# Cosine-weighted attention ahead of a routed expert layer: raw q transposed by plain products, k weighted on VectorE, and the K chunks spread evenly over the units

## The chip, the core and the metric

The kernel runs on one core of a Trainium2 chip. The metric is the device time of one execution in microseconds (us). The kernel before has a median of 337.25 us over three runs (336.64 to 337.82). The execution that was profiled took 336.46 us; its span from the first to the last instruction is 334.8 us.

Engines are named as in the profile: PE is TensorE (PEld its weight load), DVE is VectorE, ACT is ScalarE, POOL is GpSimd, SP is SyncE, which here only issues transfers.

## The reference

Eight batches of eight heads, 576 tokens of 64 values each, in float32. Attention without a softmax: q and k are rectified and weighted by a cosine and a sine of the token's place, k and v are contracted to a 128x64 matrix per head, and q is multiplied with it. Its output, 4608 rows of 512, goes through a layer in which each token uses the one of eight experts that its gate picks.

```python
def phi(x): r = np.maximum(x, 0.0); return np.concatenate([r * cos_w, r * sin_w], axis=-1)
kv  = np.einsum('bhsf,bhsd->bhfd', phi(k), v);  z = np.sum(phi(k), axis=2)
num = np.einsum('bhsf,bhfd->bhsd', phi(q), kv)
den = np.einsum('bhsf,bhf->bhs', phi(q), z)[..., None] + 1e-06
x   = num / den                                   # rows of 512: 8 heads x 64
e   = np.argmax(x @ w_gate, axis=1)               # one expert per token
out = softmax_e * sigmoid(x @ w_output_gate[:, e]) * (relu(x @ w1[e]) @ w2[e])
```

## The kernel before

Until about 158 us the kernel computes the attention, after that the expert layer. A batch of q, k or v lies in SBUF as 128 partitions x 4 head pairs x 9 chunks x 64 values: a partition holds nine neighbouring tokens of one head, and chunk c is the c-th of each nine.

**K side.** For each chunk, `kcs` holds the rectified k times the cosine (`k_cos`), and `tvs` holds v times the tangent with a column for the sum (`k_prep`). `k_piece` multiplies the two, and v itself, on PE, as 64x64 tiles; nine chunks add up in the PSUM tile `kvp`. In batches 2 to 7 both weightings are done by ACT, one chunk to an instruction (L342, L349). Then `g_cast` (DVE) and `g_keep` (ACT) copy `kvp` to SBUF, `g_tr` transposes it, and `g_mm` multiplies it with the gate weights, so that the query product yields the gate logits too.

**Q side.** A unit is a pair of chunks of one batch: four units for a batch, and a fifth after every odd batch for the ninth chunks of both. So a group, which is two batches, has nine units; there are four groups, 36 units. For a unit DVE rectifies q (`q_prep`, L492 and L496), PE transposes it as four 128x128 pieces against the identity (`q_tr`, L506), ACT copies the result out of PSUM (L509), PE multiplies with the matrix of the batch (`q_mm`, L530), ACT weights by the cosine (L535), and DVE adds the sine part (L537), which frees the PSUM tile `qo`; there are two of these. `q_out` makes the denominators on DVE and the rows of x on POOL (L556), and `route` picks experts. POOL writes the rows to their expert's place by indirect transfers (L658).

**What sets the order.** The program is written out by hand: each engine runs its instructions in the order in which the loop over the units emits them. In that loop (L975) unit i emits its own `q_mm`, the transposes of unit i + 2, the rectification of unit i + 3, the K products of the chunks that `after[i]` and `ahead[i]` list, and at its end the weightings (`preps`) for the next unit. The lists give three K chunks to a batch's first unit, two or three to the next ones, and the rest to the unit before its last. SP holds back each load of q, k or v until DVE has written the unit's `u` (L1066).

**Expert layer.** 39 slots of 128 tokens: `x_tr`, `layer1`, `h_tr`, `layer2`. The weights of the experts, 2 MB each, come through POOL's queue; the first transfer is issued behind unit 25 (L237), and DVE holds the first slots' copies back until the weights of the first two experts are there (L820).

Of the kernel before, what the change touches and what calls it, by code (L numbers as in the profile page):

```python
# [13 lines left out]
I32 = mybir.dt.int32  # L14
# [8 lines left out]
def kernel(  # L23
# [77 lines left out]
    kvcb, kvTb = own(512), own(512)  # L101
# [70 lines left out]
    def late_constants():  # L172
        DVE.tensor_copy(ident16[:], ident[:])
# [22 lines left out]

        prm_i = constp.tile([P, 6, E + 1], I32, name="prm_i")
# [9 lines left out]
        DVE.tensor_copy(prm[:], prm_i[:])  # L207
# [13 lines left out]


# [50 lines left out]
    if True:  # L273
# [59 lines left out]
        zm = wk.tile([P, 4, D], F32, name="zm", tag="zm", bufs=1)  # L333
        DVE.memset(zm[:], 0.0)
# [9 lines left out]
        def k_prep(b, cs):  # L344

            for c in cs:
                if b > 1:
                    k_cos(b, c, False)
                d = ACT.activation(tvs[:, c, :, 1:65], vbuf[b % 2][:, :, c, :], AF.Copy,  # L349
                                   scale=tanc[:, c:c + 1])  # L350
                tc.add_to_no_dep_group(f"tv{b}", d.ins)

# [27 lines left out]
        def k_piece(b, c, mh, outs, first):  # L380

            for mp in range(2):
                for i in range(2):
# [46 lines left out]
        def g_cast(b):  # L430
            for i in range(2):
                DVE.tensor_copy(kvcb[:, 256 * i:256 * i + 256].rearrange(
                    "p (m s w) -> p m s w", m=2, w=64), kv_of(b, i)[:, :, :, 0:64])

        def g_keep(b):
            new_kvm(b)
            for i in range(2):
                ACT.copy(ims(kvms[b][:])[:, i, :, :, 0:65], kv_of(b, i))

        def g0_evac(mh):  # L440
            if mh == 0:
                new_kvm(0)
            x = kvps[(0, mh)][:, :, 2:132].rearrange("p i (s w) -> p i s w", w=65)
            ACT.copy(ims(kvms[0][:])[:, :, mh, :, 0:65], x)
            DVE.tensor_copy(kvcb.rearrange("p (i m s w) -> p i m s w", i=2, m=2, w=64)[
                :, :, mh, :, :], x[:, :, :, 0:64])
# [4 lines left out]
        def g_tr(b, part=(0, 1)):  # L451
            tp = ptr.tile([P, 512], F32, name=f"kvtp{b}_{part[0]}", tag="tr")
            for qd in qds(part):
                PE.transpose(tp[:, 128 * qd:128 * qd + 128],
                             kvcb[:, 128 * qd:128 * qd + 128], ident[:])
# [29 lines left out]
        qrs = {}  # L485

        def q_prep(i):
            b, c = units[i]
            qb = qbuf[b % 2].rearrange("p m c d -> p c m d")
            if c < 4:  # L490
                qr = wk.tile([P, 2, 4, D], F32, name=f"qr{i}", tag="qr", bufs=2)
                DVE.tensor_scalar_max(qr[:], qb[:, 2 * c:2 * c + 2, :, :], 0.0)  # L492
                qrs[i] = qr
            if c == 4 or c == 3 and b % 2 == 0:
                qr = wk.tile([P, 4, D], F32, name=f"qrt{i}", tag="qrt", bufs=1)
                DVE.tensor_scalar_max(qr[:], qb[:, 8, :, :], 0.0)  # L496
                qrs[(i, 8)] = qr

        def q_tr(i):
            b, c = units[i]  # L500
            if c < 4:
                qr = qrs.pop(i)
                tp = ptr.tile([P, 512], F32, name=f"qtp{i}", tag="tr")
                for l in range(2):
                    for mh in range(2):
                        PE.transpose(toks(tp[:])[:, mh, :, l, :],  # L506
                                     qr[:, l, 2 * mh:2 * mh + 2, :].rearrange(
                                         "p m d -> p (m d)"), ident[:])
                ACT.copy(qT2[i % 2], tp[:])  # L509
            if c == 4 or c == 3 and b % 2 == 0:  # L510
                qr = qrs.pop((i, 8))
                tp = ptr.tile([P, 512], F32, name=f"qtt{i}", tag="tr")
                for mh in range(2):
                    PE.transpose(tp[:, 128 * mh:128 * mh + 128],
# [662 lines left out]
```

## Time and profile before

| | |
|---|---|
| median of three runs | 337.25 us (336.64 to 337.82) |
| profiled execution, and its span | 336.46 us, 334.8 us |
| busy over the span: PE, DVE, ACT, POOL | 286.1, 188.0, 156.4, 141.4 us |
| start, until the first unit's ACT work | 0 to 19.63 us |
| groups 0, 1, 2, 3 of the attention | 36.51, 34.30, 37.49, 30.22 us |
| from there to the end | 158.15 to 334.80 us |

A busy time is the time in which at least one instruction of the engine was under way. PE's matmuls overlap by their length in the pipeline, so a PE that reads as nine tenths busy can still have gaps; how long a row of matmuls takes is read from where it starts and where the next row starts. The stages above are cut where ACT begins with a group's first unit.

### The profile page before, as it was taken

The numbers are of one execution on the slowest core, as the hardware profiler recorded it, in microseconds if no ns is written. First come the engines' busy times: TensorE is split into PE (matmuls) and PEld (weight loads), VectorE is DVE, ScalarE is ACT, GpSimd is POOL, SyncE is SP. The second block draws the span as 40 slices with busy tenths as digits, with TensorE's granted clock in tenths as the row PEclk, the third lists the DMA queues.
The fourth block names the chain that finished last, engine by engine and source line by source line (L and its number), as shares of the span: only waits on it lengthen the run. The fifth ranks groups of instructions, "written<-read, shape, count | busy, mean of one in ns | idle before, by whom it ended". The sixth has DMA issues, their size and how long they took to land. (4 is left out here: it accounts for less than half of the span.)

```text
span 334.8 us, 10160 instructions
## 1 busy us (share of the span) xinstructions
PE 286.1 (85%) x3624; PEld 178.9 (53%) x3624; DVE 188.0 (56%) x548; ACT 156.4 (47%) x320; POOL 141.4 (42%) x184
## 2 busy tenths in 40 slices
PE   7859889888886878796958979988999999999980
PEld 3548777676665657663424545544554445444530
DVE  7484557567878989896668544434433323322330
ACT  3456889888979869752302212221232232223210
POOL 8003334328842776586677534242221322232231
PEclk9998999999999999998979999999999999999997
DMA  7997688678874877999998899999947777776811
GB/s 242 341 388 257 217 245 289 218 221 263 279 254 101 279 214 138 235 233 228 236 223 229 145 237 251 231 244 268 267 123 175 182 181 182 174 166 165 175 46 45
DMA packets 58208, 71.87 MB, mean 215 GB/s; under 512 B 23406, under 2 KB 38318, under 8 KB 58160
## 3 DMA queue, kind: packets, MB, share of 16 engines
q1 hardware_dynamic: 40608, 40.17, 42.6%
q0 software_dynamic: 17552, 31.05, 41.1%
q8 instruction: 32, 0.52, 0.7%
q14 instruction: 16, 0.13, 0.1%
HBM read 67.61 MB, written 16.17 MB: 250 GB/s over the span
## 5 line engine op out<-in xcount | busy, mean ns | idle before, releaser
L860 ACT ACTIVATE hs<-hp 128x1024 f16<-128x1024 f32 x39 | 39.9, 1023 | 118.3 <-PE hp L852 118.3
L852 PE MATMUL hp<-wt,xts 128*128 x312 | 75.3, 385 | 3.1 <-DVE xts L820 1.9
L870 PE MATMUL yps<-wt,hts 128*128 x312 | 74.9, 384 | 3.0 <-DVE ysb L877 1.5
L877 DVE TENSOR_SCALAR ysb<-yps,xg 128x512 f32<-128x512 f32 x39 | 29.3, 751 | 82.4 <-PE yps L870 82.4
L881 POOL DMA_INDIRECT out_dram<-ysb,sidx x31 | 30.2, 974 | 84.0 <-DVE ysb L877 81.9
L530 PE MATMUL qo<-kvm,wt 64*64 64x162 f32 x1024 | 43.4, 306 | 12.6 <-DVE wt L537 5.5
L870 PEld LDWEIGHTS <-hts 128*128 128x128 f16 x312 | 30.8, 99 | 40.9 <-issue 3.6
L537 DVE SCALAR_TENSOR_TENSOR wt<-qo,sinq,wt 128x324 f32<-128x324 f32 x72 | 36.8, 549 | 21.9 <-ACT wt L535 17.3
L852 PEld LDWEIGHTS <-xts 128*128 128x128 f16 x312 | 29.4, 99 | 32.2 <-issue 3.1
L535 ACT ACTIVATE wt<-qo,cosq 128x324 f32<-128x324 f32 x72 | 35.9, 536 | 17.6 <-PE qo L530 17.4
L530 PEld LDWEIGHTS qo<-kvm,wt 64*64 64x64 f32 x1024 | 34.9, 134 | 17.1 <-DVE wt L537 8.0
L392 PE MATMUL kvp<-wt 64*64 64x132 f32 x1080 | 38.3, 278 | 5.1 <-ACT wt L349 2.6
L556 POOL TENSOR_TENSOR xr<-wt,rc 128x512 f16<-128x512 f32 x36 | 38.0, 1062 | 6.4 <-DMA xs<-xr,di@1_0_1857 5.4
L392 PEld LDWEIGHTS kvp<-wt 64*64 64x64 f32 x1080 | 29.9, 132 | 12.4 <-ACT wt L349 7.1
L349 ACT ACTIVATE wt<-wt,tanc 128x256 f32<-128x256 f32 x63 | 31.6, 513 | 0.2 <-DMA wt<-in_v_dram 0.2
L573 POOL TENSOR_TENSOR gl<-wt,rc 128x256 f32<-128x256 f32 x12 | 7.6, 631 | 51.1 <-DVE rc L548 39.0
L342 ACT ACTIVATE wt<-wt,cosc 128x256 f32<-128x256 f32 x54 | 28.0, 518 | 0.0
L506 PE MATMUL qtp<-ident,qr 128*128 128x128 f32 x128 | 21.2, 288 | 3.7 <-DVE qr L492 2.0
L820 DVE COPY xts<-xtsp 128x512 f16<-128x512 f16 x39 | 16.3, 419 | 14.3 <-PE xtsp L804 4.8
L509 ACT COPY wt<-qtp 128x512 f32<-128x512 f32 x32 | 18.9, 589 | 5.9 <-PE qtp L506 5.7
L492 DVE TENSOR_SCALAR qr<-wt 128x512 f32<-128x512 f32 x32 | 19.6, 615 | 0.5 <-PE qtp L506 0.5
L506 PEld LDWEIGHTS qtp<-ident,qr 128*128 128x128 f32 x128 | 14.0, 143 | 8.9 <-DVE qr L492 3.4
(275 smaller groups left out, 303.3 us busy)
## 6 DMA issues: line engine op xcount, KB each, us to landing
wt<-in_moe_w_dram POOLq DMA_DIRECT2D x16, 1024.0 KB, 14.4
wt<-in_k_dram SPq DMA_DIRECT2D x16, 576.0 KB, 5.9
wt<-in_v_dram SPq DMA_DIRECT2D x16, 576.0 KB, 5.6
wt<-in_q_dram SPq DMA_DIRECT2D x16, 576.0 KB, 7.1
xg<-xs SPq DMA_DIRECT2D x43, 129.0 KB, 3.3
xs<-zt SPq DMA_DIRECT2D x9, 129.0 KB, 5.8
out_dram<-ysb,sidx POOLq DMA_INDIRECT x31, 2.9
hts<-hs SPq DMA_TRANSPOSE x19, 3.7
```

Source lines behind the costliest of these rows:

```text
L349: d = ACT.activation(tvs[:, c, :, 1:65], vbuf[b % 2][:, :, c, :], AF.Copy, scale=tanc[:, c:c + 1])
L392: mm = PE.matmul(outs(i, mp), kcs[rows, m, c, :], mov, start=first, stop=(c == NCH - 1), skip_group_check=True)
L506: PE.transpose(toks(tp[:])[:, mh, :, l, :], qr[:, l, 2 * mh:2 * mh + 2, :].rearrange("p m d -> p (m d)"), ident[:])
L530: PE.matmul(qo[64 * l:64 * l + 64, 2 * mp + ih, 0:162], qT[r, hf, ih, l, :], kvms[b if c < 4 else b - 1 + l][r, n0:n0 + 2, :], start=True, ...
L535: d0 = ACT.activation(t, qo[:, :, 0:81], AF.Copy, scale=cosq[:, c:c + 1])
L537: d1 = DVE.scalar_tensor_tensor(u[:, h0:h0 + 4, :], qo[:, :, 81:162], sinq[:, c:c + 1], t, ALU.mult, ALU.add)
L556: GP.tensor_tensor(xrows[:, slot + x, 0:DM].bitcast(F16).rearrange("p (h d) -> p h d", d=D), u[:, 8 * x:8 * x + 8, 0:64], rc[:, 8 * x:8 * ...
L852: mm = PE.matmul(hp[:, fh * 512:fh * 512 + 512], xts[:, kc, :], wt[:, bass.ds(ev, 1), kc * F + fh * 512:kc * F + fh * 512 + 512], start=(k ...
L860: ACT.activation(hs[:], hp, AF.Relu)
L870: mm = PE.matmul(yp, hts[:, fc, :], wt[:, bass.ds(ev, 1), 4 * F + fc * DM:4 * F + fc * DM + DM], start=(fc == 0), stop=(fc == 7))
L877: DVE.tensor_scalar(ysb[:], yp, xg[:, DM + 2:DM + 4].bitcast(F32), None, ALU.mult)
L881: d = GP.indirect_dma_start(out=out[:, :], out_offset=bass.IndirectOffsetOnAxis(ap=idx, axis=0), in_=ysb[:], in_offset=None, bounds_check= ...
```

## The change

- `q_prep` is gone. PE takes q as it was loaded: instead of four transposes of 128x128, `turn` makes eight plain products with the identity as the moving operand, each giving 64 of the 128 output partitions. ACT rectifies while it copies out of PSUM.
- `k_cos` runs on DVE for all batches from 1 on, once for all chunks of a unit: one instruction that takes the larger of k and zero and multiplies by a table `cosw` of 128x576, which POOL fills at the start. The weighting of v stays on ACT, but one chunk is given to DVE before the fourth and the ninth unit of a group.
- `g_cast` is gone. `g_keep` copies half of `kvp` on ACT and half on DVE, and `g_tr` transposes that copy, again by `turn`.
- The K chunks are spread over all units, mostly two to a unit, starting two units before the end of the group before for odd batches. The copy out of PSUM moves to the unit after the last chunk.
- Nine weightings of batch 1 and the constants that stood on DVE ahead of unit 0 are split: one weighting of two chunks stays there, the others go behind units 0 and 1, the constants into unit 4.
- Loads of q, k and v are issued up to two units earlier in a group; zeroed rows go out two to a unit; `q_sum` moves into `q_out`; the steps of the rank and table computation are dealt out differently.

```diff
-        def k_cos(b, c, dve):
-            kc = kbuf[b % 2][:, :, c, :]
-            if dve:
-                DVE.scalar_tensor_tensor(kcs[:, :, c, :], kc, cosc[:, c:c + 1], zm[:],
-                                         ALU.mult, ALU.max)
-            else:
-                ACT.activation(kcs[:, :, c, :], kc, AF.Relu, scale=cosc[:, c:c + 1])
+        def k_cos(b, cs):
+            c0, c1 = cs[0], cs[-1] + 1
...
+            DVE.scalar_tensor_tensor(
+                flat(kcs), flat(kbuf[b % 2]), 0.0,
+                cosw[:, c0 * D:c1 * D].unsqueeze(1).to_broadcast([P, 4, (c1 - c0) * D]),
+                ALU.max, ALU.mult)
...
+            for x, c in enumerate(cs):
+                v_, t_ = vbuf[b % 2][:, :, c, :], tvs[:, c, :, 1:65]
+                if x < on_dve:
+                    d = DVE.tensor_scalar(t_, v_, tanc[:, c:c + 1], None, ALU.mult)
+                else:
+                    d = ACT.activation(t_, v_, AF.Copy, scale=tanc[:, c:c + 1])
...
-            for i in range(2):
-                ACT.copy(ims(kvms[b][:])[:, i, :, :, 0:65], kv_of(b, i))
+            for i, copy in enumerate((ACT.copy, DVE.tensor_copy)):
+                copy(ims(kvms[b][:])[:, i, :, :, 0:65], kv_of(b, i))
...
+        def turn(out, in_):
+            PE.matmul(out, in_, ident[:], start=True, stop=True)
...
                 for l in range(2):
                     for mh in range(2):
-                        PE.transpose(toks(tp[:])[:, mh, :, l, :],
-                                     qr[:, l, 2 * mh:2 * mh + 2, :].rearrange(
-                                         "p m d -> p (m d)"), ident[:])
-                ACT.copy(qT2[i % 2], tp[:])
+                        for mp, to in enumerate(halves):
+                            turn(toks(tp[:])[to, mh, :, l, :],
+                                 qb[:, 2 * mh + mp, 2 * c + l, :])
+                ACT.activation(qT2[i % 2], tp[:], AF.Relu)
...
+            for b, plan in ((2 * g + 1, {-2: [0, 1], -1: [2, 3], 0: [4, 5], 1: [6, 7, 8]}),
+                            (2 * g + 2, {2: [0, 1], 3: [2, 3], 4: [4, 5], 5: [6, 7], 6: [8]})):
...
+                        after[9 * g + n] = (b, w)
...
-                step({20: 1, 21: 2, 22: 3, 23: 0, 24: 3, 25: 0, 26: 0}.get(i, 1))
+                step({20: 1, 21: 2, 22: 1, 23: 1, 24: 2, 25: 2}.get(i, 1))
```

DVE's order at the start, from the copy of the second half of batch 0 to the first unit's L537, in the kernel before:

```order
L477 COPY kvm_247<-kvgp_1_345 128x2x2x16
L339 SCALAR_TENSOR_TENSOR wt<-wt,cosc,zm 128x4x64 x9
L173 CAST ident_110<-ident 128x128
L186 CAST iota_114<-iota_i 128x8
L187 TENSOR_SCALAR iota8m<-iota_114 128x8
L188 TENSOR_SCALAR reg_116<-iota_114 128x8
L191 CAST iota_117<-iota_i 128x9
L194 CAST pv<-pv_i 128x1
L207 CAST prm<-prm_i 128x54
L209 TENSOR_TENSOR low<-iota_114 128x64
L213 TENSOR_TENSOR lt<-iota_114 128x64
L216 COPY base<-reg_116 128x8
```

And now, where `wt,cosw` marks the new weighting and L529 is the line that was L537:

```order
L480 COPY kvm_251<-kvgp_1_351 128x2x2x16
L339 SCALAR_TENSOR_TENSOR wt<-wt,cosw 128x4x128
L529 SCALAR_TENSOR_TENSOR wt<-qo_0_390,sinq,wt 128x324
L529 SCALAR_TENSOR_TENSOR wt<-qo_1_401,sinq,wt 128x324
L339 SCALAR_TENSOR_TENSOR wt<-wt,cosw 128x4x192
```

Nineteen instructions stood between that copy and the first unit's L537; one is left, and the other weightings follow behind.

ACT's order over one unit in the middle of a group, before, from one unit's two L535 to the next unit's (L342 and L349 weight k and v):

```order
L535 ACTIVATE wt<-qo_1_682,cosq 128x324
L509 COPY wt<-qtp_694 128x512
L342 ACTIVATE wt<-wt,cosc 128x4x64
L349 ACTIVATE wt<-wt,tanc 128x4x64
L342 ACTIVATE wt<-wt,cosc 128x4x64
L349 ACTIVATE wt<-wt,tanc 128x4x64
L535 ACTIVATE wt<-qo_0_735,cosq 128x324
```

The same place now (L527 is the former L535, L502 the former L509, L353 weights v):

```order
L527 ACTIVATE wt<-qo_0_1031,cosq 128x324
L527 ACTIVATE wt<-qo_1_1042,cosq 128x324
L502 ACTIVATE wt<-qtp_1053 128x512
L353 ACTIVATE wt<-wt,tanc 128x4x64 x3
L527 ACTIVATE wt<-qo_0_1093,cosq 128x324
```

The weightings of k have left ACT's queue.

PE's order over units 6 and 7, before (L530 is the query product, L514 and L506 the transposes of q, L454 that of the K matrix, L392 the K product):

```order
L530 MATMUL qo_1_807<-kvm_601,wt 64x162 x8
L514 MATMUL qtt_819<-ident,qrt_763 128x128 x2
L392 MATMUL kvp_702<-wt 64x132 x32
L530 MATMUL qo_0_867<-kvm_601,wt 64x162 x8
L530 MATMUL qo_1_878<-kvm_601,wt 64x162 x8
L454 MATMUL kvtp_0_889<-ident,wt 128x128 x4
L506 MATMUL qtp_895<-ident,qr_823 128x2x64 x4
```

The same two units now, and the K product behind unit 7 (L522 is the query product, L489 every `turn`, L399 the K product):

```order
L522 MATMUL qo_1_827<-kvm_595,wt 64x162 x8
L489 MATMUL qtt_838<-ident,wt 64x128 x4
L399 MATMUL kvp_648<-wt 64x132 x24
L522 MATMUL qo_0_880<-kvm_595,wt 64x162 x8
L522 MATMUL qo_1_891<-kvm_595,wt 64x162 x8
L489 MATMUL kvtp_0_902<-ident,kvm_877 64x128 x8
L489 MATMUL qtp_912<-ident,wt 64x2x64 x8
L399 MATMUL kvp_922<-wt 64x132 x16
```

Every piece to be transposed is now two products, and unit 7, which had no K product, has one of the next batch.

## Rows read from the trace of the kernel before

**Rows 1.** Busy time by stage: us, PE, PEld, DVE, ACT, POOL, PEclk, DMA share, GB/s.

```profile
19.63:56.14 36.51, 30.56 (x686) 25.39 (x682) 22.36 (x67) 28.41 (x67) 11.62 (x13) 0.95 0.82 262
56.14:90.44 34.30, 29.40 (x672) 23.43 (x668) 24.01 (x67) 29.69 (x73) 18.82 (x23) 1.00 0.79 250
90.44:127.93 37.49, 28.97 (x656) 22.97 (x649) 31.96 (x96) 30.28 (x73) 22.51 (x25) 1.00 0.68 214
127.93:158.15 30.22, 24.81 (x486) 18.62 (x485) 25.60 (x76) 19.00 (x46) 19.91 (x22) 0.98 1.11 215
...
175.00:334.80 159.80, 143.74 (x866) 73.08 (x863) 61.34 (x154) 36.83 (x36) 49.68 (x53) 0.99 0.81 184
```

**Rows 2.** ACT in order of time, group 1: start, us, line, tile.

```profile
70.75 0.51 ACT L342 ACTIVATE wt<-wt,cosc 128x256 f32<-128x256 f32 x1
...
73.17 0.93 ACT L535 ACTIVATE wt<-qo,cosq 128x324 f32<-128x324 f32 x2
```

**Rows 3.** Waits of groups 1 and 2: engine, line, waited for; us, times, longest.

```profile
PEld kvp L392 <- ACT wt L349: 4.0, 10, 0.8
...
PE qo L530 <- DVE kvm L475: 2.5, 1, 2.5
```

**Rows 4.** PE in order of time, group 1: start, us until the last result.

```profile
77.22 1.13 PE L392 MATMUL kvp<-wt 64*64 64x132 f32 x32
78.17 1.28 PE L530 MATMUL qo<-kvm,wt 64*64 64x162 f32 x32
79.39 0.44 PE L514 MATMUL qtt<-ident,qrt 128*128 128x128 f32 x2
...
84.48 0.60 PE L506 MATMUL qtp<-ident,qr 128*128 128x128 f32 x4
85.01 1.33 PE L530 MATMUL qo<-kvm,qTt 64*64 64x162 f32 x32
86.27 0.66 PE L469 MATMUL kvgp<-wpr,wt 128*64 128x32 f32 x16
```

**Rows 5.** PE's L469 under way or done by 86.34 us, by 86.37 us.

```profile
86.27 0.25 PE L469 MATMUL kvgp<-wpr,wt 128*64 128x32 f32 x2
86.27 0.31 PE L469 MATMUL kvgp<-wpr,wt 128*64 128x32 f32 x4
```

**Rows 6.** DVE's groups in group 1: count, busy us, mean ns, idle before.

```profile
L492 DVE TENSOR_SCALAR qr<-wt 128x512 f32<-128x512 f32 x8 | 4.3, 543 | 0.0
...
L432 DVE COPY wt<-kvp 128x256 f32<-128x256 f32 x4 | 1.5, 418 | 1.2 <-PE kvp L392 1.1
...
L496 DVE TENSOR_SCALAR qrt<-wt 128x256 f32<-128x256 f32 x2 | 1.5, 736 | 0.0
```

**Rows 7.** The same line L492 in group 2.

```profile
L492 DVE TENSOR_SCALAR qr<-wt 128x512 f32<-128x512 f32 x8 | 6.1, 760 | 0.0
```

**Rows 8.** L573 on DVE over the span: ns min/median/max.

```profile
L573 DVE TENSOR_TENSOR gl<-wt,rc x8: 291/425/1771, 55.1 to 166.2; 128x128 f32<-128x128 f32 x4, 128x256 f32<-128x256 f32 x4
```

**Rows 9.** DVE in order of time, ahead of unit 0 and in it.

```profile
18.56 3.65 DVE L339 SCALAR_TENSOR_TENSOR wt<-wt,cosc,zm 128x256 f32<-128x256 f32 x9 [0.41 <-DMA wt<-in_k_dram]
...
23.19 1.01 DVE L537 SCALAR_TENSOR_TENSOR wt<-qo,sinq,wt 128x324 f32<-128x324 f32 x2
24.12 0.41 DVE L492 TENSOR_SCALAR qr<-wt 128x512 f32<-128x512 f32 x1
```

**Rows 10.** PE in order of time, units 1 and 3.

```profile
23.79 2.29 PE L530 MATMUL qo<-kvm,wt 64*64 64x162 f32 x32 [3.09 <-DVE wt L537]
...
33.43 1.28 PE L530 MATMUL qo<-kvm,wt 64*64 64x162 f32 x32
```

**Rows 11.** ACT's first weighting of v of batch 1.

```profile
21.61 1.30 ACT L349 ACTIVATE wt<-wt,tanc 128x256 f32<-128x256 f32 x3 [0.24 <-DMA wt<-in_v_dram]
```

**Rows 12.** POOL: the first transfer of expert weights.

```profile
127.23 0.83 POOL L237 DMA_DIRECT2D wt<-in_moe_w_dram  x1
```

**Rows 13.** DVE: the first slots' copies, held back for the weights.

```profile
156.48 0.75 DVE L820 COPY xts<-xtsp 128x512 f16<-128x512 f16 x2 [2.23 <-DMA wt<-in_moe_w_dram]
```

More of the change, by code (lines that the diff above doesn't have):

```diff
@@ L100 @@
     kbuf[1] = mcd(own(HW))
-    kvcb, kvTb = own(512), own(512)
+    kvTb = own(512)
     qbuf[0] = mcd(own(HW))
@@ L206, in late_constants @@
         GP.memset(prm_i[:, 5, E:E + 1], E - 1)
+        for m, i in ((GC, 0), (GC, 1), (4, 1), (5, 1)):
+            t = constp.tile([P, m + 1, E], F16, name=f"oh16_{m}_{i}")
+            GP.memset(t[:, m, :], 0.0)
+            oh16s[(m, i)] = t
+    def late_constants():
+        DVE.tensor_copy(ident16[:], ident[:])
+        DVE.tensor_copy(iota8[:], iota8_i[:])
+        DVE.tensor_scalar_add(iota8m[:], iota8[:], -8.0)
+        DVE.tensor_scalar_mul(reg0[:], iota8[:], float(REG))
+        DVE.tensor_copy(iota9[:], iota9_i[:])
+        DVE.tensor_copy(pv[:], pv_i[:])
         DVE.tensor_copy(prm[:], prm_i[:])
@@ L331, in place_gates, with flat, k_prep @@
                             :, :, 2 * ab:2 * ab + 2, :])
-        zm = wk.tile([P, 4, D], F32, name="zm", tag="zm", bufs=1)
-        DVE.memset(zm[:], 0.0)
-        def k_cos(b, c, dve):
-            kc = kbuf[b % 2][:, :, c, :]
-            if dve:
-                DVE.scalar_tensor_tensor(kcs[:, :, c, :], kc, cosc[:, c:c + 1], zm[:],
-                                         ALU.mult, ALU.max)
-            else:
-                ACT.activation(kcs[:, :, c, :], kc, AF.Relu, scale=cosc[:, c:c + 1])
[L344 to L350, printed above, removed]
+        cosw = wk.tile([P, NCH * D], F32, name="cosw", tag="cosw", bufs=1)
+        def k_cos(b, cs):
+            c0, c1 = cs[0], cs[-1] + 1
+            def flat(x):
+                return x[:, :, c0:c1, :].rearrange("p m c d -> p m (c d)")
+            DVE.scalar_tensor_tensor(
+                flat(kcs), flat(kbuf[b % 2]), 0.0,
+                cosw[:, c0 * D:c1 * D].unsqueeze(1).to_broadcast([P, 4, (c1 - c0) * D]),
+                ALU.max, ALU.mult)
+        def k_prep(b, cs, on_dve):
+            if b > 1:
+                k_cos(b, cs)
+            for x, c in enumerate(cs):
[4 more added lines that the diff above has]
+                    d = ACT.activation(t_, v_, AF.Copy, scale=tanc[:, c:c + 1])
                 tc.add_to_no_dep_group(f"tv{b}", d.ins)
+                for x_ in range(NCH):
+                    if x_ != c:
+                        tc.declare_no_dep(d.ins, group=f"mm{b - 1}_{x_}",
+                                          reason="of another chunk")
         def k0_prep(hf):
@@ L443, in g0_evac @@
             x = kvps[(0, mh)][:, :, 2:132].rearrange("p i (s w) -> p i s w", w=65)
-            ACT.copy(ims(kvms[0][:])[:, :, mh, :, 0:65], x)
-            DVE.tensor_copy(kvcb.rearrange("p (i m s w) -> p i m s w", i=2, m=2, w=64)[
-                :, :, mh, :, :], x[:, :, :, 0:64])
+            for i, copy in enumerate((ACT.copy, DVE.tensor_copy)):
+                copy(ims(kvms[0][:])[:, i, mh, :, 0:65], x[:, i])
         def qds(part):
@@ L453, in g_tr @@
             for qd in qds(part):
-                PE.transpose(tp[:, 128 * qd:128 * qd + 128],
-                             kvcb[:, 128 * qd:128 * qd + 128], ident[:])
+                for s in range(2):
+                    turn(tp[64 * s:64 * s + 64, 128 * qd:128 * qd + 128],
+                         kvms[b][:, 2 * qd + s, 0:64])
             def pick(x):
@@ L483, in toks @@
             return x.rearrange("p (m i l t) -> p m i l t", m=2, i=2, l=2)
[L485 to L497, printed above, removed]
+        def turn(out, in_):
+            PE.matmul(out, in_, ident[:], start=True, stop=True)
         def q_tr(i):
             b, c = units[i]
+            qb = qbuf[b % 2]
+            halves = (slice(0, 64), slice(64, 128))
             if c < 4:
-                qr = qrs.pop(i)
                 tp = ptr.tile([P, 512], F32, name=f"qtp{i}", tag="tr")
@@ L949 @@
         g_tr(0, (1,))
-        q_prep(0)
-        q_prep(1)
         q_tr(0)
-        q_prep(2)
         g_mm(0, (1,))
-        q_tr(1)
-        for c in range(NCH):
-            k_cos(1, c, True)
-        late_constants()
+        k_cos(1, [0, 1])
+        pool_constants()
         pending = []
@@ L1068 @@
                 f(*x)
-            if 3 <= i <= 3 + E:
-                zero_rows(i - 3)
+            if 3 <= i <= 7:
+                for e in range(2 * i - 6, min(2 * i - 4, E + 1)):
+                    zero_rows(e)
             if i == 19:
```

100 lines of the change are left out of this document (42 added, 58 removed).

## The prediction

> **What bounds it now.** I read the busy times by stage first [rows 1]. From 175 us on PE is busy 143.7 of 159.8 us; the change touches nothing there, so any gain has to come from the attention, 19.63 to 158.15 us. In groups 0 and 1 the fullest engine beside PE is ACT (28.4 of 36.5 us, 29.7 of 34.3), in group 2 DVE (32.0 of 37.5) with ACT close behind (30.3). In group 3 the DMA share is 1.11.
>
> PE's 29 us per group are not a measure, since its records overlap. The order of time shows what PE needs when nothing holds it [rows 4]: 32 K products (two chunks) 0.95 us from their start to the next start (77.22 to 78.17), a unit's 32 query products 1.22 with the changeover behind them (78.17 to 79.39), four transposes 0.53 with the changeover back (84.48 to 85.01), which I split into 0.44 and 0.09; 16 gate products 0.59 (the busy 0.66 less the end of the last one). A group has nine units, 18 K chunks, eight sets of four and two of two for q, two of four for kv, two gate products: 9 x 1.22 + 9 x 0.95 + 8 x 0.44 + 2 x 0.22 + 2 x 0.44 + 2 x 0.59 + 9 x 0.09 for the changeover back + about 0.3 for the ranks = 26.6 us. Group 1 took 34.3, so PE waits nearly 8 us in it. The waits say for whom [rows 3]: K products for ACT's v, the query product for the gate columns. ACT is the common cause: in units with three chunks it runs six weightings in a row, 0.40 us from start to start (70.75 to 73.17) [rows 2], with the next unit's L535 behind them.
>
> **ACT.** 18 L342 a group at 0.40 us, 7.2 us [rows 2], leave its queue; two weightings of v and half of the copies out of `kvp` go too. ACT falls to about 21 of 34 us and bounds nothing. Relu in place of a plain copy out of PSUM I take as free: L342, a Relu, has the same spacing as the weighting of v beside it [rows 2].
>
> **PE.** A set of four transposes becomes eight products of 64 columns. Each is two records, as every plain float32 product here (the order lists 16 L392 for two chunks, the trace 32), and streams 128 columns. Per set of four tiles 132 columns take 0.95/8 = 0.119 us with the end of the row, so 128 take about 0.11. Whether the two 64-column halves run beside each other decides: beside, 8 pairs x 0.11 = 0.89 us; in a row, 16 x 0.11 = 1.78. The one row of that shape is the gate product: by 86.34 us two have started, by 86.37 four [rows 5], so they start in pairs. I take 0.89, 0.45 more than now, and keep 0.44 and 1.78 as ends. A group then needs 26.6 + 8 x 0.45 + 2 x 0.22 + 2 x 0.45 - 0.2 (gate products and transposes no longer change over) = 31.3 us. That is the new floor, below each of the three groups' times.
>
> **DVE.** Removed in group 1: L492, L496 and L432, 4.3 + 1.5 + 1.5 = 7.3 us [rows 6]. Added: nine weightings for 18 chunks. One chunk now takes 0.40 (3.65 us for nine, the last result included) [rows 9]; DVE's tensor products grow by about 1.05 ns per element (128 to 256 elements, 291 to 425 ns) [rows 8], so two chunks take 0.67, three 0.93. One triple, seven pairs and a single are 6.0 us; two copies at 0.36 and two weightings of v, for which I take 0.3 each, make 7.3. DVE stays at 24 us in group 1 and 31 in group 2 (where 6.1 of L492 go [rows 7]). The bounds for one pair: 0.41, what DVE's fastest form needs for 512 elements, and 0.75 plus a wait for POOL (rival 1).
>
> That wait is real today. L492 takes 0.41 us alone [rows 9], 0.54 on average in group 1 and 0.76 in group 2 [rows 6, 7], where POOL is busy 22.5 us; L573 takes 1.77 us at worst instead of 0.29 [rows 8]. I let the nine weightings inherit what L492 pays now, so it cancels.
>
> The Trainium skill, "SBUF — State Buffer", section "Who interferes with whom", says that a VectorE instruction with two SBUF inputs is blocked for the whole of a GpSimd instruction that reads SBUF; the new weighting has two, k and `cosw`. L573, also with two, agrees; by this rule alone each weighting could pay a full wait, which is rival 1.
>
> **The start.** PE waits 3.09 us in unit 1 for L537 [rows 10], which stands behind the nine weightings and the constants until 23.19 [rows 9]. With one pair ahead of it (0.75 us from 18.56) it follows L535 at about 20.2. What is late next is v of batch 1: its first weighting waits for the transfer until 21.61 [rows 11], the first K product comes at 22.4, unit 1's query product at 23.4 instead of 23.79. From there to unit 3 PE needs 2 x 1.22 + 2 x 0.98 + 0.44 + 7 x 0.475 = 8.2 us against 9.64 now (23.79 to 33.43; the query product there took 2.29 us instead of 1.28) [rows 10]. So unit 3 starts 1.9 us earlier. Units 3 to 8 have little to gain: PE's sum for them comes to about 22 us, as long as they take now. Start and group 0: -2.0 us.
>
> **Groups 1 and 2.** With even K chunks ACT and DVE have their work for a unit done before PE wants it, and the gate columns get a K product's time to arrive; PE's waits go, its own sum stays. Group 1: 31.3 plus 0.7 of remaining waits, 32.0, -2.3 us. In group 2 the rank and table steps sit on DVE in lumps, and DVE has 31 us of work beside PE's 31.3; I take the middle between 31.3 and 37.5, 34.4. Eight ninths of that gain fall ahead of the first weight transfer: -2.7.
>
> **Group 3 and the end.** The first transfer of weights starts at 127.23 [rows 12], and the first slots wait for weights until 156.48 [rows 13], with the DMA engines full [rows 1]. These 29.3 us are bytes, not engine time; I carry them over unchanged, and all that follows. The gain is what unit 25 gains. PE and DVE will be done earlier in group 3 and wait longer.
>
> **At nothing.** `cosw` is made on POOL while the first loads run and is first wanted at 18.6 [rows 9]; I put its worst at 1 us. Zeroed rows two to a unit and loads one or two units earlier go past SP's hold on `u`; groups 0 and 1 have a DMA share of about 0.8. Worst 1 us in group 0. The reduction of the gate sums moves behind a POOL result that is then two units old.
>
> **Sum.** -2.0 - 2.3 - 2.7 = -7.0 against the profiled 336.46: 329.5 us. The median shown is 0.8 above that execution, so 330.3 in its terms.
>
> **Rivals.** 1. Slower: the weightings collide with POOL. If each of nine waits out a POOL instruction, 1.77 - 0.29 = 1.48 us, DVE has 24.0 + 13.3 = 37.3 us in group 1 and 44.4 in group 2: +3.0, +6.9 x 8/9, less 2.0 at the start (POOL is idle there) = +7.1, 344. It decides from a wait of (34.3 - 24.0)/9 = 1.1 us each in group 1. For it speaks the 1.77, against it the means of L492, 0.13 and 0.35 above its undisturbed time. Chance 0.11.
> 2. Slower: the halves don't overlap. PE then has 31.3 + 12 x 0.89 - 0.9 = 41 us a group: +6.7, +3.2, and some 7 in group 0: 353. Against it the pairs in [rows 5]. Chance 0.04.
> 3. It trades one wait for another: PE's longer turns and DVE's weightings fill what ACT sets free, groups 1 and 2 stay near their times, the start remains: 335.3, spread 333 to 338. Speaks for it: DVE at 32 of 37.5 keeps all its work. Chance 0.17.
> 4. More: the weights land earlier too, because fewer other bytes are under way when they start, and group 3 (PE's own sum there, by the same prices, is about 26 of 30.2 us) gives back 4 us: 326. Against it the DMA share of 1.11. Chance 0.15.
> The forecast itself has 0.53, with 327 to 334.
>
> **Numbers.** Under 0.3% (1 us) a measurement of this kernel can't tell a difference from none. Faster: 0.53 + 0.15 + 0.10 of rival 3 = 0.78; same 0.07; slower 0.11 + 0.04 = 0.15. The range 324 to 337.5 leaves out rivals 1 and 2 and the edges of 3 and 4, under 0.2.
>
> **What would show it.** Turns of eight products that last 0.9 us (1.8 would be rival 2); pair weightings of 0.75 us, under 1.1 on average (2.2: rival 1); group 1 in 32 us with ACT busy about 21; no wait of 3 us in unit 1; the first slots' wait for weights longer than 2.2 us and still 29 us behind the first transfer. Wrong it is if group 1 takes 34 us or more, or if the attention's gain is lost in the wait for weights.

## The result and the profile after

The kernel after takes 340.48 us (median of 20 runs, 335.64 to 342.75), the kernel before 336.53 us beside it (20 runs, 333.59 to 339.34): 1.0103 of its time, 95% interval 1.0069 to 1.0137. It is slower by 1.0%. (The ratio leaves out executions that took over 1.5% more than their kernel's fastest; the medians of all 20 stand at 1.0117.) I had forecast 330.3 us and 324 to 337.5. The profiled execution of after has a span of 339.0 us, 4.2 more than that of before.

The windows of after by stage, cut where the first ScalarE weighting of units 0, 9, 18 and 27 starts and the last unit's result ends, as in [rows 1] (width, then busy us and count of PE, weight loads, DVE, ACT, POOL, clock, DMA share, GB/s):

```profile
18.95:57.02 38.07, 35.55 (x872) 31.03 (x868) 24.18 (x59) 25.69 (x55) 14.12 (x14) 1.00 0.84 291
57.02:91.90 34.88, 32.65 (x802) 28.25 (x798) 26.12 (x67) 22.99 (x51) 20.52 (x21) 1.00 0.66 229
91.90:129.80 37.90, 33.01 (x802) 28.15 (x798) 34.63 (x96) 23.37 (x50) 23.54 (x25) 1.00 0.58 198
129.80:161.68 31.88, 27.31 (x537) 20.81 (x530) 24.80 (x70) 16.39 (x35) 20.15 (x21) 1.00 1.10 209
175.00:338.00 163.00, 148.99 (x877) 75.55 (x875) 61.38 (x154) 36.91 (x37) 52.21 (x55) 0.97 0.83 184
```

Every group is longer than in [rows 1]: +1.56, +0.58, +0.41 and +1.66, together +4.21 us. That is one execution of each. The same program, run again as experiment 9, took 37.6, 34.8 and 39.2 us in groups 0 to 2, and experiment 8, whose group 1 is that of after, took 37.2 us in it. So no single group's difference is shown by these rows; their sum fits the medians. Unit 0 starts 0.68 earlier (19.63 to 18.95), and from the last unit's end to the end of the span it is 177.3 us instead of 176.7. The same rows say how the four groups grew. PE is busy 128.5 us in them instead of 113.7, 14.8 more. The time in which it is not busy falls from 24.8 to 14.2 us, 10.6 less. So waits did go, but fewer than half of them where I had forecast nearly all, and more PE work came in than waits went out. ACT fell from 29.7 to 23.0 us in group 1, much as forecast, and the group got no shorter.

PE of after in order of time, two units of group 1 (start, us, what):

```profile
70.17 1.28 PE L522 MATMUL qo<-kvm,wt 64*64 64x162 f32 x32
71.38 0.66 PE L472 MATMUL kvgp<-wpr,wt 128*64 128x32 f32 x16
71.87 1.07 PE L489 MATMUL qtp<-ident,wt 128*64 128x128 f32 x16
72.87 1.13 PE L399 MATMUL kvp<-wt 64*64 64x132 f32 x32
```

A turn takes 1.00 us from its start to the next start (71.87 to 72.87); four transposes took 0.53 (84.48 to 85.01 in [rows 4]). That is 0.47 more a unit, where I had 0.45. The Trainium skill, "Perfetto Trace Analysis", section "Transposes", says that a logical transpose should use the transpose operation rather than a plain matrix product; the trace agrees, by these 0.47 us. It speaks against this change, and I had not weighed it.

The waits of after, of group 1 first (us in total, times, longest) and then of group 2:

```profile
ACT wt L527 <- PE qo L522: 4.5, 9, 0.9
DVE wt L529 <- ACT wt L527: 2.9, 3, 1.1
...
PE kvtp L489 <- DVE kvm L441: 0.7, 1, 0.7
```

```profile
ACT wt L527 <- PE qo L522: 4.9, 8, 1.1
...
PE kvtp L489 <- DVE kvm L441: 2.7, 2, 2.0
PE kvp L399 <- DVE wt L339: 2.1, 3, 1.2
```

No product of PE waits for ACT any more in these two groups; ACT now waits for PE's query product in most units. In group 2 PE is idle for 4.89 us, and 4.8 of them are waits for DVE, for its half of the kv copy and for the new weighting of k. In group 1 PE is idle for 2.23 us, in three places ("issue" is a pause for which the profile names nothing that was waited for):

```profile
58.61 1.09 PE L489 MATMUL qtp<-ident,wt 128*64 128x128 f32 x16 [1.11 <-issue]
67.76 0.66 PE L489 MATMUL kvtp<-ident,kvm 128*64 128x128 f32 x8 [0.71 <-DVE kvm L441]
75.50 0.49 PE L522 MATMUL qo<-kvm,wt 64*64 64x162 f32 x5 [0.42 <-issue]
```

So two thirds of what was left are pauses of the first kind. Group 1 of the kernel before had them too:

```profile
PE kvp L392 <- issue: 1.0, 1, 1.0
PE qtp L506 <- issue: 0.7, 1, 0.7
```

That weighting over the whole kernel (min, median, max ns), and then DVE and POOL around the longest unit, 25:

```profile
L339 DVE SCALAR_TENSOR_TENSOR wt<-wt,cosw x29: 410/682/2303, 18.5 to 135.3; 128x512 f32<-128x512 f32 x21, 128x768 f32<-128x768 f32 x5, 128x256 f32<-128x256 f32 x2, 128x1024 f32<-128x1024 f32 x1
```

```profile
121.86 0.68 DVE L339 SCALAR_TENSOR_TENSOR wt<-wt,cosw 128x512 f32<-128x512 f32 x1
122.47 0.42 DVE L441 COPY kvm<-kvp 128x260 f32<-128x260 f32 x1
...
125.44 1.55 DVE L339 SCALAR_TENSOR_TENSOR wt<-wt,cosw 128x512 f32<-128x512 f32 x1
```

```profile
124.80 0.63 POOL L566 TENSOR_TENSOR gl<-wt,rc 128x256 f32<-128x256 f32 x1 [2.02 <-DVE glog L573]
125.39 1.06 POOL L549 TENSOR_TENSOR xr<-wt,rc 128x512 f16<-128x512 f32 x1
...
128.89 0.83 POOL L235 DMA_DIRECT2D wt<-in_moe_w_dram  x1
```

Two chunks take 0.68 us in the first row and 1.55 where POOL's L549 began 0.05 us earlier. Of the 21 weightings of two chunks five took over 1 us (1.05 to 2.30), each with an L549 under way in it. The last line is the first transfer of weights, 1.66 later than in [rows 12]. The copies that wait for it start at

```profile
160.00 0.75 DVE L813 COPY xts<-xtsp 128x512 f16<-128x512 f16 x2 [2.35 <-DMA wt<-in_moe_w_dram]
```

31.1 us behind it, against 29.3 from [rows 12] to [rows 13]. They wait for the weights of two experts, and POOL issues the second expert's first transfer 12.6 us behind the first expert's (11.6 before, 127.23 to 138.82), after a wait for DVE's denominators:

```profile
139.30 2.29 POOL L549 TENSOR_TENSOR xr<-wt,rc 128x512 f16<-128x512 f32 x2 [6.29 <-DVE rc L540]
141.53 0.82 POOL L235 DMA_DIRECT2D wt<-in_moe_w_dram  x1
```

So about 1 of these 1.8 us comes from the order of the engines and not from the transfers.

### The profile page after: what moved, and what is told of

Same layout as the page of the kernel before. It is cut to its first block, busy times and chain, and to the rows that moved or that the text cites. A ratio compares the mean times of both kernels' runs of the same rounds, so it can differ in the third digit from the quotient of the medians.

```text
span 339.0 us, 11125 instructions
## 1 busy us (share of the span) xinstructions
PE 300.8 (89%) x4152; PEld 197.6 (58%) x4152; DVE 193.2 (57%) x526; ACT 136.7 (40%) x253; POOL 147.7 (44%) x185
## 3 DMA queue, kind: packets, MB, share of 16 engines
q1 hardware_dynamic: 40608, 40.17, 41.1%
## 5 line engine op out<-in xcount | busy, mean ns | idle before, releaser
L853 ACT ACTIVATE hs<-hp 128x1024 f16<-128x1024 f32 x39 | 39.9, 1023 | 118.3 <-PE hp L845 118.3
L863 PE MATMUL yps<-wt,hts 128*128 x312 | 76.1, 388 | 1.7 <-DVE ysb L870 1.5
L870 DVE TENSOR_SCALAR ysb<-yps,xg 128x512 f32<-128x512 f32 x39 | 29.3, 750 | 83.9 <-PE yps L863 83.9
L527 ACT ACTIVATE wt<-qo,cosq 128x324 f32<-128x324 f32 x72 | 37.4, 530 | 20.8 <-PE qo L522 20.2
L529 DVE SCALAR_TENSOR_TENSOR wt<-qo,sinq,wt 128x324 f32<-128x324 f32 x72 | 36.9, 548 | 14.2 <-ACT wt L527 10.2
L522 PE MATMUL qo<-kvm,wt 64*64 64x162 f32 x1024 | 43.1, 299 | 2.0 <-issue 1.0
L399 PE MATMUL kvp<-wt 64*64 64x132 f32 x1080 | 38.0, 277 | 6.9 <-ACT wt L353 2.2
L549 POOL TENSOR_TENSOR xr<-wt,rc 128x512 f16<-128x512 f32 x36 | 39.6, 1106 | 6.6 <-DVE rc L540 6.3
L399 PEld LDWEIGHTS kvp<-wt 64*64 64x64 f32 x1080 | 30.4, 132 | 12.8 <-issue 7.2
L522 PEld LDWEIGHTS qo<-kvm,wt 64*64 64x64 f32 x1024 | 35.2, 132 | 4.5 <-issue 2.4
L489 PE MATMUL qtp<-ident,wt 128*64 128x128 f32 x512 | 34.5, 277 | 1.1 <-issue 1.1
L566 POOL TENSOR_TENSOR gl<-wt,rc 128x256 f32<-128x256 f32 x12 | 9.4, 786 | 55.2 <-DVE glog L573 20.3
L489 PEld LDWEIGHTS qtp<-ident,wt 128*64 128x64 f32 x512 | 27.8, 137 | 5.1 <-issue 5.1
L502 ACT ACTIVATE wt<-qtp 128x512 f32<-128x512 f32 x32 | 19.1, 596 | 17.7 <-PE qtp L489 16.8
L353 ACT ACTIVATE wt<-wt,tanc 128x256 f32<-128x256 f32 x57 | 25.7, 501 | 0.4 <-DVE wt L339 0.4
L339 DVE SCALAR_TENSOR_TENSOR wt<-wt,cosw 128x512 f32<-128x512 f32 (+3 forms) x29 | 25.1, 866 | 0.6 <-DMA wt<-in_k_dram 0.6
L797 PE MATMUL xtsp<-ident,xg 128*128 128x128 f16 x156 | 15.2, 222 | 3.6 <-DMA xg<-xs 3.6
```

The lines of the kernel that those rows point to most:

```text
L353: d = ACT.activation(t_, v_, AF.Copy, scale=tanc[:, c:c + 1])
L399: mm = PE.matmul(outs(i, mp), kcs[rows, m, c, :], mov, start=first, stop=(c == NCH - 1), skip_group_check=True)
L489: PE.matmul(out, in_, ident[:], start=True, stop=True)
L522: PE.matmul(qo[64 * l:64 * l + 64, 2 * mp + ih, 0:162], qT[r, hf, ih, l, :], kvms[b if c < 4 else b - 1 + l][r, n0:n0 + 2, :], start=True, ...
L527: d0 = ACT.activation(t, qo[:, :, 0:81], AF.Copy, scale=cosq[:, c:c + 1])
L529: d1 = DVE.scalar_tensor_tensor(u[:, h0:h0 + 4, :], qo[:, :, 81:162], sinq[:, c:c + 1], t, ALU.mult, ALU.add)
```

## The experiments

The kernel before was run in every job, and its median went from 336.5 to 343.4 us between jobs. So I compare ratios, and kernels of one job with each other where I can. But the other kernels moved less: experiments 12 and 13 are the same kernel in two jobs, 334.14 and 334.54 us, and experiment 6, which lacks two small edits of theirs, took 334.62 where before took 343.18. A ratio to a before of 343 us is therefore too favourable, and after itself was never run beside one. Theory A: PE's own added work bounds groups 0 and 1, DVE's weighting groups 2 and 3. Theory B: DVE's weighting alone is the cause.

**1. The price of the turn.**

```diff
-  for mp, to in enumerate(halves):
-      turn(toks(tp[:])[to, mh, :, l, :], qb[:, 2 * mh + mp, 2 * c + l, :])
+  PE.transpose(toks(tp[:])[:, mh, :, l, :],
+               qb[:, 2 * mh + l, 2 * c:2 * c + 2, :].rearrange("p c d -> p (c d)"), ident[:])
```

> The kernel after, but each 128x128 block of q is turned by one whole-width transpose of 128 contiguous columns (two chunks of one head) in place of two 64-wide products; the data land in the wrong arrangement, so the output is not the reference's, while every other instruction and every transfer is as in the kernel after. Theory A (TensorE's own work sets the pace: the turn of 16 records takes 0.82 us a unit where four transposes took 0.38 to 0.44): 32 units x 0.43 plus 8 tail blocks x 0.17 = 15 us come off TensorE, part of it returns as waits; 326 to 333 us, group 1 at 30 to 33 us. Theory B (VectorE's wide k weighting beside GpSimd sets the pace, 25 us of it at a mean of 866 ns): not more than 2 us gained, 337 us or more.

Measured 357.06 us, 1.0565 (1.0505 to 1.0626). The total can't be read here: the wrong rows are routed unevenly, and from the start of unit 35 to the end it takes 203 us instead of 181. The attention can: units 0 to 35 take 133.6 us instead of 139.2. Its windows:

```profile
18.68:54.68 36.00, 32.12 (x752) 27.62 (x748) 24.59 (x58) 25.85 (x55) 13.88 (x14) 0.95 0.91 295
54.68:86.40 31.72, 29.03 (x694) 24.33 (x690) 25.55 (x68) 22.99 (x50) 19.69 (x21) 1.00 0.74 253
86.40:125.53 39.13, 31.12 (x694) 25.64 (x690) 35.81 (x98) 23.26 (x51) 25.29 (x27) 0.96 0.63 203
```

Groups 0 and 1 get 2.1 and 3.2 us shorter, group 2 gets 1.2 longer: theory A in the first two, and something else, with DVE busy 35.8 us, in the third.

**2. The turn alone, in the kernel before.** The same eight products and Relu in the copy; VectorE's `q_prep` taken out.

> The kernel before with one part of the change: raw q turned by products of 64 columns and rectified in ScalarE's copy, VectorE's rectifying copy gone; k weighting, kv copies, K stream, loads and start as before. Theory A: TensorE gains 15 us of work over 32 units, its waits of 32 us in the four groups hide part of it; 340 to 346 us against 336.5, TensorE's floor in group 1 from 26.7 to 30.6 us. Theory B: the turn is hidden and VectorE is relieved of 8 copies of about 0.54 us a group: 332 to 336.5 us.

Four runs, 339.48 to 345.55 us, median 343.14 against 336.91, without an interval: within theory A's forecast. The profiled one has 36.0 us in group 1 (34.3 before) and 37.4 in group 2 (37.5). The turn is not hidden, and DVE's relief returns nothing in groups 0 and 1.

**3. k weighted on ScalarE again, in the kernel after.**

```diff
-  DVE.scalar_tensor_tensor(flat(kcs), flat(kbuf[b % 2]), 0.0, ..., ALU.max, ALU.mult)
+  for c in cs:
+      ACT.activation(kcs[:, :, c, :], kbuf[b % 2][:, :, c, :], AF.Relu, scale=cosc[:, c:c + 1])
```

> The kernel after, but k is weighted chunk by chunk on ScalarE again (one activation of 128x256 a chunk), so that VectorE sheds 25 us of weighting and ScalarE takes up some 28 us. Theory A: TensorE's floor of 31.7 us in group 1 stays, and so do 337 to 345 us. Theory B: the pace was VectorE's: 328 to 335 us.

336.89 us beside 336.91, 0.9971 (0.9921 to 1.0021): between the two forecasts. Group 1 is not shorter than in after (35.7 us), groups 2 and 3 are (36.7 and 30.0). Each theory holds for half the program, as far as one execution tells.

**4. The pairs made by the load.** q written as `p (c m d)`, in runs of 64 floats, and four whole transposes of raw q.

> The kernel after with q laid out by its load so that the two heads of a pair stand side by side (written in runs of 64 floats), and raw q turned by four whole transposes a unit; still rectified in ScalarE's copy. The output is the reference's. Theory A: as the whole-width turn, 326 to 333 us, if the transfers of 256-byte runs stay hidden; if they do not, waits for q appear in the first units of a batch and the time is 340 us or more. Theory B: 337 us or more without any wait for q.

344.67 us, 1.0212 (1.0157 to 1.0267). The loads don't stay hidden. The queue of the loads (packets, MB, share of the engines' time), and the longest wait for one, in units 10 and 11:

```profile
q1 hardware_dynamic: 73632, 40.17, 46.1%
```

```profile
ACT wt L358 <- DMA wt<-in_v_dram: 6.1, 1, 6.1
```

The bytes are those of after, in 73,632 packets instead of 40,608, and 46.1% of the engines' time instead of 41.1%. It is v, behind q in the same queue, that comes 6.1 us late. SP shows part of the way: it takes 6.47 us over issuing the four transfers of q ahead of it, where after takes 0.90 over its two, and this v goes out at 60.28 us instead of 54.72 (unit 8 starts at 54.9 instead of 53.4).

```profile
48.78 6.47 SPq L296 DMA_DIRECT2D wt<-in_q_dram  x4
60.28 0.43 SPq L299 DMA_DIRECT2D wt<-in_v_dram  x1
```

```profile
47.51 0.90 SPq L292 DMA_DIRECT2D wt<-in_q_dram  x2
54.72 0.37 SPq L292 DMA_DIRECT2D wt<-in_v_dram  x1
```

**5. The turn undone, the weighting kept.** `q_prep` and the transposes of before put into the kernel after.

> The kernel after with the turn of q undone: VectorE rectifies q into a copy and four whole transposes turn it, as in the kernel before (the rectified copies lie in two tiles placed anew); VectorE's k weighting, the turn of kv, the even K stream, loads and start stay. Theory A (TensorE's own work sets the pace in groups 0 and 1, VectorE's in 2 and 3): TensorE sheds 15 us, but VectorE takes up 8 copies of some 0.55 us a group on top of 26 us in group 1 and 35 in group 2; groups 0 and 1 each 1 to 3 us shorter than after, group 2 at 40 us or more, 338 to 346 us in all. Theory B (VectorE's k weighting sets the pace everywhere): VectorE is loaded further, every group longer, 348 us or more.

342.61 beside 343.18, 0.9964 (0.9929 to 1.0). Group 2 takes 43.4 us with DVE busy 39.1; group 0 is 1.1 shorter than in after, group 1 0.1. Theory A's forecast for the groups, except for group 1.

**6. The even stream without both.** Experiments 3 and 5 together.

> The kernel after with both the turn of q and VectorE's k weighting undone (q rectified on VectorE and transposed whole; k weighted chunk by chunk on ScalarE): what stays of the change is the even stream of K chunks, the one kv copy on two engines with its own turn, the loads and the start. Theory A: TensorE's floor in group 1 is some 27.7 us again and VectorE's about 23, ScalarE at 30 us with its work spread evenly; 328 to 334 us, group 1 at 32 to 33 us. Theory B (the even stream, the kv copy or the loads are what costs): 337 us or more.

334.62 beside 343.18, 0.9713 (0.9654 to 0.9772): faster than before, and than experiments 5, 7 and 8 beside it (341.69 to 344.02 us), which keep one part or both.

**7, 8. Two small places.** In 7, `g_tr(cast[i])` stands behind `q_tr(i + 2)`; in 8, the step table is `{22: 3, 23: 0, 24: 3, 25: 0, 26: 0}`.

> The kernel after with one pair of calls exchanged: TensorE turns the q block of two units on before it turns a batch's kv, so that VectorE's half of the kv copy has the time of a q turn (0.8 us) to end. Theory A: the 0.97 us that the kv turn waits in group 1 and 3.27 us in group 2, with VectorE's copy named, fall by about 0.8 us a batch, 1 to 4 us in all: 336.5 to 339.5 us. Theory B: the order of the two turns is not on the path, 340 to 341 us.

> The kernel after with only the table of routing steps of group 2 put back ({22: 3, 23: 0, 24: 3, 25: 0, 26: 0}). Unit 25 takes 6.3 us after (4.0 before) with VectorE busy for 6.8. Theory A: the two steps at unit 25 are what makes it long; they return to 24, unit 25 falls to some 4 to 5 us and group 2 as a whole by 0 to 2 us, 338 to 341 us. Rival: the work is only moved, unit 24 grows by what unit 25 loses, within 1 us of after.

0.9962 (0.9924 to 1.0) and 1.0017 (0.9981 to 1.0053). After itself wasn't in that job, so whether 7 gained can't be settled; their intervals touch. In the trace of 7 the wait ahead of kv's turn is gone in group 1 and 1.2 us in group 2, where after has 2.7. In 8, unit 25 falls from 6.3 to 5.8 us and unit 23 grows from 3.2 to 4.8: the work is moved, as the rival says, though to 23 and not to 24.

**9 to 12. One job: after, the copy's halves, the old K plan, the best so far.** In 10, `declare_no_dep` between the two halves of `g_keep`; in 11, experiment 6 with

```diff
-  {-2: [0, 1], -1: [2, 3], 0: [4, 5], 1: [6, 7, 8]}
+  {0: [0, 1, 2], 1: [3, 4, 5]}   # and [6, 7, 8] ahead of the query product of unit 2
```

(the even batches likewise); in 12, experiment 6 with the edits of 7 and 10.

> The kernel after itself, beside the others of this job, so that they can be compared with it on one chip. Both theories: 1.007 to 1.014 of before, as in the first comparison.

> The kernel after, but VectorE's half of the kv copy no longer waits for ScalarE's half (they write different columns; so far the second stands behind the first). Theory A: the wait of TensorE's kv turn (0.97 us in group 1, 3.27 in group 2) falls by 0.4 us a batch, the time of ScalarE's half; 0.5 to 2.5 us shorter than the kernel after on this chip, TensorE's floor and most of its waits stay. Rival: the wait is for VectorE's queue, not for ScalarE; no difference (within 0.3%).

> The kernel with the even stream alone, but the K chunks stand where the kernel before has them (three, three and three, or three, two, two and two, the last ones ahead of a unit's query product); kv copy, kv turn, loads and start stay new. Theory A: the even stream is what gains; the time goes back to 0.99 to 1.00 of before. Rival: the gain is from the loads, the start and the single kv copy; 0.97 to 0.98 of before.

> The kernel with the even stream alone, and in it the kv turn behind the next q block and VectorE's half of the kv copy freed of ScalarE's. Theory A: 0.96 to 0.97 of before, 1 to 3 us under the even stream alone. Rival: these waits are not on the path where TensorE is not the bound; the same as the even stream alone, 0.97 to 0.98.

After 1.0124 (1.004 to 1.0208); halves apart 1.0137 (1.003 to 1.0243); old K plan 1.0133 (1.0043 to 1.0223); the even stream with both small edits 0.9946 (0.99 to 0.9992). The intervals of the first two are too wide for the 0.5 to 2.5 us in question, but the trace of 10 has in group 2 the same wait as after, so it is for DVE's queue and not for ACT's half:

```profile
PE kvtp L491 <- DVE kvm L442: 2.7, 2, 2.0
```

11 lies above both of its forecasts, and so does 12. From 11 to 12 it is 5.6 us. Beside the K plan, and the place of the kv copy that goes with it, 11 lacks the two small edits, and two weightings of v a group are back on ACT (29.8 us busy in group 1, 28.4 in 12). The small edits are not the gain: experiment 6, without them, took 334.62 us, as long as 12 and 13. The two weightings were not tried apart. So the even plan carries the gain, all or most of it; and with the old plan what else is left of the change (the loads, the start, the one kv copy and its turn) is 1.3% slower than before. Group 1 with the old plan, its width and then two of its waits:

```profile
57.18:91.58 34.40, 29.92 (x698) 24.35 (x691) 23.07 (x65) 29.78 (x72) 19.92 (x22) 1.00 0.69 240
```

```profile
PEld kvp L398 <- ACT wt L352: 3.0, 4, 1.7
PE kvp L398 <- ACT wt L352: 2.2, 2, 1.6
```

This is the wait of [rows 3] for ACT's v again, with 34.4 us as in [rows 1]. In 12 and 13 group 1 takes 31.0 and 31.5 us.

**13 to 16. A square on one job.** All with the edits of 12: neither the turn nor the weighting, the turn, the weighting, both.

> Square of four kernels on one chip, all with the even stream, the kv turn behind the next q block and the halves of the kv copy apart. This one has neither the turn of q nor VectorE's k weighting. Both theories: the fastest of the four, 0.97 to 0.995 of before.

> The square: raw q turned by products and rectified on ScalarE, k weighted on ScalarE. Theory A (TensorE's 4.7 us a group of added work is on the path in every group whose waits are short): 4 to 8 us slower than neither, group 1 at 35 us with waits of 3 us. Theory B (only VectorE's weighting costs): within 2 us of neither.

> The square: q rectified on VectorE and transposed, k weighted on VectorE. Theory A': the weighting alone costs where VectorE is full, in groups 2 and 3 (39 us busy in group 2): 4 to 8 us slower than neither, nearly all behind unit 18. Theory B': it costs evenly in all groups.

> The square: both, the kernel after with the two small edits. Theory A: the two take the place of each other's waits, so that both cost about as much as the dearer one plus 1 to 4 us; 6 to 10 us slower than neither. Rival: they add up, 10 to 15 us slower than neither; or q off VectorE makes room for the weighting, and both cost less than the weighting alone.

| | k on ACT | k on DVE |
|---|---|---|
| q transposed | 334.54 us, 0.9885 (0.9846 to 0.9923) | 340.6, 1.007 (1.0033 to 1.0106) |
| q turned | 337.42, 0.998 (0.995 to 1.0011) | 340.2, 1.0083 (1.0045 to 1.0122) |

Groups 1 and 2 of the four, as windows, in the order neither, turn (this profiled execution took 2.9 us more than its median), weighting, both:

```profile
56.79:88.29 31.50, 29.36 (x691) 24.54 (x687) 23.82 (x69) 28.19 (x69) 19.13 (x22) 1.00 0.77 267
88.29:122.19 33.90, 29.85 (x687) 24.23 (x686) 32.06 (x93) 28.98 (x69) 21.76 (x25) 1.00 0.65 223
```

```profile
57.03:92.59 35.56, 33.41 (x796) 28.66 (x794) 19.80 (x59) 29.05 (x70) 19.20 (x22) 1.00 0.69 242
92.59:127.24 34.65, 32.89 (x804) 28.23 (x798) 29.45 (x85) 28.98 (x69) 21.61 (x24) 1.00 0.63 217
```

```profile
54.05:86.70 32.65, 29.39 (x694) 24.36 (x690) 30.74 (x78) 23.04 (x51) 19.63 (x21) 1.00 0.74 255
86.70:126.62 39.92, 29.93 (x694) 24.41 (x690) 37.82 (x105) 23.16 (x51) 24.52 (x26) 1.00 0.59 192
```

```profile
57.35:90.31 32.96, 32.19 (x803) 28.25 (x799) 26.60 (x67) 23.03 (x51) 19.69 (x21) 1.00 0.70 240
90.31:128.18 37.87, 33.00 (x802) 28.14 (x797) 34.88 (x95) 23.43 (x51) 23.86 (x25) 1.00 0.60 202
```

The turn alone costs 2.9 us by the medians, less than theory A's 4 to 8 and more than theory B's 2. In these executions it is 4.1 us in group 1, where DVE has room and PE then is nearly full (33.4 of 35.6), though with the weighting beside it group 1 takes 33.0. The weighting costs 6.0 us in group 2, where DVE then is (37.8 of 39.9). Both together, 5.7 us by the medians, cost no more than the weighting alone (6.1): with q off DVE the weighting has 3 us more room in group 2. So the weighting by itself accounts for the loss, and beside it the turn costs nothing that the total shows. The two don't add up, as expected of A; that both cost less than the weighting in group 2 is the rival's part.

**17. The weighting on DVE only for batches up to 4.** Experiment 15 with `if b >= 5` back on ScalarE.

> The kernel of the square without the turn, with k weighted on VectorE for the batches up to 4 (whose weightings fall in groups 0 and 1) and on ScalarE for batches 5 to 7 (groups 2 and 3). Theory A: the weighting costs only where VectorE is full; unit 18 starts at 86 to 88 us and the rest runs as without the weighting, 0.98 to 0.99 of before (331 to 334 us where before is 337). Rival: the weighting costs everywhere, 1.00 of before or more.

334.91 beside 343.42, 0.9755 (0.9705 to 0.9804). The rival is out: where DVE has room the weighting costs nothing that the total shows, and unit 18 to unit 35 take 61.1 us, as in 13. But unit 18 starts at 91.8 us, not at 86 to 88; units 14 and 17 are long here (4.6 and 4.2 us, 2.8 and 3.3 in 15). In unit 17 k is weighted on ACT again, for batch 5. In unit 14 nothing differs from 15, and experiment 5 took 4.6 us there as well; why is not settled. It is faster than the kernel before beside it (which took 343 us), and is not shown to beat experiment 6 or 13.

## Why the prediction was wrong

The step that failed is "PE's waits go, its own sum stays". The work that was added to PE came at about its price. The waits that were to pay for it went only in part (10.6 of 24.8 us in the four groups): some had not been waits for ACT, and new ones, for DVE, took the place of others, most of all in group 2. In the square the kernel with neither part is 3.2 us below before, the one with both 2.5 above. By its own sign, a group 1 of 34 us or more, the prediction was wrong.

- **The turn** was right in size: 0.47 us against 0.45 a unit, the halves side by side (rival 2 is out).
- **PE's new floor** of 31.3 us was nearly right: of the 34.9 us of group 1 some 2.8 are pauses by PE's starts, which leaves 32.1, and group 1 of experiment 16, which has both parts and both small edits, takes 32.96 with PE busy 32.2.
- **The weighting** was right in size: 0.68 us a pair in the median against 0.75, 0.87 on average, under the 1.1 of rival 1. Its sum was not. The weightings were to inherit what L492 pays for POOL, "so it cancels"; but the 4.3 and 6.1 us that were taken out hold that payment, and the 7.3 put in do not. With L492 taken out at its 0.41 us, 8 x 0.41 + 3.0 = 6.3, the same figures give 25.0 and 33.0 us for groups 1 and 2, not 24 and 31. DVE stands at 26.1 and 34.6.
- **ACT** fell to 23 us against 21. "ACT is the common cause" was read from waits for its results, and so the freeing of ACT was booked as part of the gain. With the even plan it isn't needed. With neither part, ACT is busy 28.2 us in group 1, nearly as before (29.7), and the group takes 31.5 us, while after, with ACT at 23.0, it takes 34.9. The even plan removes the waits for ACT though ACT keeps its work, and the old plan brings them back (experiment 11): PE's next operand stood behind six weightings in a row. That even chunks help, the prediction had said too; the weightings of k taken off ACT then gained nothing more in total, and were paid for on DVE (6.1 us in the square). Whether freeing ACT would have helped with the old plan, no run shows.
- **Group 1**, 31.3 plus 0.7 of waits, came to 34.88, about 32.1 plus 2.8. Some 1.5 us of PE's idle time are pauses without a cause in the profile, and the kernel before had 1.7 of them: the 0.7 I left had no room even for these. Another 0.7 is DVE's kv copy.
- **Group 2**: the middle of 31.3 and 37.5 became 37.90, above its upper end. DVE's k weighting is what holds it (39.9 against 33.9 us in the square, 37.9 against 34.7 with the turn); I had counted its work, 2 us too low, and given the waits for DVE half, where they are nearly all of PE's idle time.
- **Group 0**: "as long as they take now" for units 3 to 8 came to 23.7 us against 21.1. PE's sum of 22 for them was itself 0.9 above what they take now, and again left nothing for waits (PE is idle for 2.5 us in the group). The start was right up to unit 3 (1.7 us earlier, forecast 1.9), and all of it was given back by unit 9. Part of that start is TensorE's clock: in the kernel before PE was busy 0.21 of the 2 us ahead of 24 us, and from 24 to 26 us the granted clock was 0.50, the lower level, which is the query product of 2.29 us in [rows 10]; in after it was 1.00 throughout.
- **The tail** moved with the attention, but the weights took 31.1 us instead of 29.3. They were not all "bytes, not engine time": 1 us is POOL's later issue of the second expert.
- Of the rivals, 3 names the mechanism, one wait traded for another, and its 335.3 us had only gains in it.

What stays open: how much the loads, the start and the one kv copy give or take one by one; what the pauses are that the profile gives no cause for; and why group 1 of the same code takes 34.8 us in one execution and 37.2 in another.

## What to carry to other kernels

A wait for an engine says that its result came late, not that the engine has too much to do: before work is moved off it, even out its order, and see whether the wait goes. An engine's own sum is the least a stage can take; where a change fills that engine to 90%, book at least the pauses of before for which no engine is named, and ask which engine the added work makes late, rather than book nothing. Parts of a change that move load to different engines should be weighed stage by stage, since the engine with room in one stage (DVE in group 1) is the full one in the next.

## What the runs showed that I had not expected

- Four transposes against sixteen records of plain products: the same data, 0.53 and 1.00 us. I had computed it, and still not seen that without the weighting the turn gives back 2.9 of the 3.2 us that the even plan gains in the square.
- q in runs of 256 bytes delays not q but what SP issues behind it: v comes 6.1 us late (experiment 4).
- The kernel before differs by 2% between jobs (336.5 to 343.4 us), while the kernel with neither part was at 334.1 to 334.6 us in three of them (experiments 6, 12 and 13).
- The same kernel's groups differ between executions: group 0 took 34.2 us in experiment 12 and 37.4 in 13, where the granted clock was 0.50 for a stretch of it (24 to 26 us).
